# Loading v in two transfers of 64 rows instead of one from a two-block source, in a fused RWKV and convolutional FFN kernel

## The chip, the cores and the metric

One core of a Trainium2 chip. The metric is the device time of one execution in microseconds (us). Three runs of the kernel before gave 355.97, 357.77 and 359.85 us, median 357.77.

## What is computed

For 4 batches and 8 heads of width 48, over 768 steps, a linear attention with a state of 48x48 per head; its output, 384 wide, then goes through a gated FFN with a convolution of three taps along the sequence:

```python
for t in range(S):
    kt, vt, rt = (k[:, :, t], v[:, :, t], r[:, :, t])
    cur = np.einsum('bhd,bhe->bhde', u[None] * kt, vt)
    y[:, :, t] = np.einsum('bhd,bhde->bhe', rt, state + cur)
    state = w[None, :, :, None] * state + np.einsum('bhd,bhe->bhde', kt, vt)
...
h = np.maximum(x @ w_in, 0.0)
conv_out += conv_w[k][None, None, :] * hp[:, k:k + S, :]     # k = 0, 1, 2
gate = 1.0 / (1.0 + np.exp(-conv_out))
return (h * gate @ w_out).astype(np.float32)
```

## The kernel before

The sequence is cut into 24 groups of 128 steps (6 for each batch), a group into two chunks of 64. Each group g is first prepared (`prep`): DVE scales k and r of the group in `KR` by tables of decay powers that stand in PSUM (`TKR`, a view of `PO[2]`, built once at the start); for groups below 11 PE makes a token-major copy of k (line 453) which ACT puts into `TOK` (line 463), and sums for the diagonal (line 461); from group 11 on (`NE`) that copy comes from HBM as `krt` and POOL or DVE multiply it. From group 11 (`GP`) the scaling reads `TKS`, a copy of the tables in SBUF made once by ACT (line 376; the trace calls that tile TKR).

Then comes a visit (`visit`, lines 488 to 560). On PE it makes the masked scores of the next group (line 516, into `SP`), the state update k by v of the next group (line 525, into `UP`) and the outputs of this group (lines 521 and 527, into `AV`). So line 525 needs v of group g+1 in `TOK`, line 527 v of group g. After a visit DVE masks the scores and adds the states, POOL multiplies the states by the decay (`MM`), and ACT and DVE split the output in a high and a low part into `XT` (line 555 and the `tt` behind it). From group 3 on six small DMAs of 16 rows each move a part of `XT` from partition to partition.

The FFN goes over 7 units of up to 462 columns, 8 slices of 128 hidden rows each: 9 matmuls a slice for the first layer (line 585), relu, convolution, gate and split on ACT, DVE and POOL (lines 591 to 602), and 9 for the second (line 626). The first slice needs the first three groups. The weights come as 64-bit words that ACT, DVE and POOL turn to floats in 16 pieces of 384 KB and one small one (`convert`, three buffers `ST`); these are spread over the first unit.

The order of all instructions is made before the launch by a planner (`Plan`): each operation is given with an engine, an estimated duration, what it reads and writes and, for a DMA, an estimate `x` of the transfer. The planner works its own due times out and emits one fixed order for each engine; it also puts in dummy matmuls on `wz` (line 699). On the chip each engine goes through its order and waits in place. Nearly all DMAs are issued from one queue, SP's, so a DMA that waits holds up every one behind it; three loads of `KR` at the start are issued by ACT.

The loads of a group are made by `load`: two transfers for `KR` (k and r, 64 or 48 rows each), from group 11 on one for `krt` (384 KB), and one for v of 192 KB. In HBM v of a group lies in a block of 128 rows with zeros in two of four quarters, so the 128 rows that are wanted start at two places: rows 0 to 63 in the first half of the columns and rows 64 to 127 in the second. The source is therefore written by hand as an access pattern of three steps, 2 blocks by 64 rows by 384 elements, while the destination is 128 rows by 384 elements.

Of the kernel before, what the change touches and what calls it, by code (L numbers as in the profile page):

```python
# [14 lines left out]
B, H, S, D = 4, 8, 768, 48  # L15
DM, DF = 384, 1024
C = 64
NP = H // 2
# [43 lines left out]
class Plan:  # L62
# [11 lines left out]
    def op(self, eng, dur, rd, wr, fn, cls="", x=0.0, port=False, mode=0, dma=False):  # L74
        n = len(self.ops)
        self.dma.append(dma)
        pred = set()
        for k in rd:
            if k in self.last_w:
                pred.add(self.last_w[k])  # L80
        for k in wr:
            if k in self.last_w:
                pred.add(self.last_w[k])
            pred.update(self.last_r.get(k, ()))
        for k in rd:
            self.last_r.setdefault(k, []).append(n)
        for k in wr:
            self.last_w[k] = n
            self.last_r[k] = []
        pred.discard(n)  # L90
        if not isinstance(dur, dict):
            dur = {eng: dur}
        cls = cls or (wr[0] if isinstance(wr[0], str) else wr[0][0])
        self.ops.append((dur, x, sorted(pred), fn, cls, mode))
        self.port.append(port)
        return n
# [134 lines left out]
def rwkv_ffn_kernel(tc, krd, krt, vt, wd, ut, w_in, conv_w, w_out, out):  # L231
    nc = tc.nc
    V, A, G, SP, PE = nc.vector, nc.scalar, nc.gpsimd, nc.sync, nc.tensor
    plan = Plan()
    op = plan.op
    with ExitStack() as ctx:
# [3 lines left out]
        def sb(shape, dt, name, n=None):  # L240
            if n is None:
                return cst.tile(shape, dt, name=name)
            return [cst.tile(shape, dt, name=f"{name}{i}") for i in range(n)]
# [3 lines left out]
        TOK = sb([128, 3, NP, 2, D], F32, "TOK", NBUF)  # L247
        SC = sb([128, NP, 2, C], F32, "SC", 2)
# [17 lines left out]
        TKS = sb([112, 2, NP, C], F32, "TKR")  # L266
# [9 lines left out]
        TKR = PO[2][0:112].rearrange("q (a p t) -> q a p t", a=2, p=NP)  # L276
# [17 lines left out]
        def dma(rd, wr, dst, src, dur=0.5, x=0.1, cls="", q="sp"):  # L294
            op(q, dur, rd, wr, lambda e: e.dma_start(dst, src), cls, x, dma=True)  # L295
# [11 lines left out]
        def kr(i):  # L307
            return [(n, i, x) for n in ("KK", "RR") for x in range(2)]
# [3 lines left out]
        def load(g, q="sp"):  # L312
            i = g % NBUF
            dst = KR[i].rearrange("q a p t -> q (a p t)")
            n = 64 if g < NBUF else D
            dma([], [(n_, i, 0) for n_ in ("KK", "RR")], dst[0:n], rows[g * 112 + 64:g * 112 + 64 + n], 0.45, 0.63, "ldK")
            dma([], [(n_, i, 1) for n_ in ("KK", "RR")], dst[64:64 + D], rows[g * 112:g * 112 + D], 0.45, 0.63, "ldK", q)
            if g >= NE:
                dma([], [("tK", i), ("tR", i)], TOK[i][:, 0:2], krt[g], 0.45, 1.3, "ldT")
            a = vt[g]  # L320
            v = bass.AP(a.tensor, a.offset, [[(64 * 2 + 1) * NP * 2 * D, 2], [2 * NP * 2 * D, 64], [1, NP * 2 * D]])
            dma([], [("tV", i)], TOK[i][:, 2].rearrange("q p c d -> q (p c d)"), v, 0.45, 0.65, "ldV")

        load(0, "act")
        dma([], ["uu"], uu, ut, 0.45, 0.4, "ldU")
        op("pool", 0.1, [], ["ident"], lambda e: G.memset(ident, 1.0))
# [23 lines left out]
        TKK = ["TK1", "TK2", "TR1", "TR2"]  # L350
# [22 lines left out]
        op("pool", 0.6, ["w64", "ident"], ["D64"], lambda e: G.tensor_tensor(  # L373
            out=D64, in0=ident.unsqueeze(1).broadcast_to([112, NP, D]), in1=w64.broadcast_to([112, NP, D]), op=ALU.mult))
        op("pe", 0.4, ["uu", "eye"], ["AV"], ucol, "ucol", 100, mode=1)
        op("act", 0.55, TKK, ["TKS"], lambda e: A.copy(TKS, TKR), "TKS")
        su_ = AV.rearrange("q p c t -> q (p c t)")[0:112, 0:NP].unsqueeze(2)
        op("dve", 0.2, ["AV", "PW"], ["uw"], lambda e: V.tensor_tensor(out=uw.unsqueeze(2), in0=su_, in1=PW[:, :, 1:2], op=ALU.mult))

        def decays():  # L380
            op("dve", 0.6, ["PW", "PW0"], ["PL"], powers2)
            op("act", 0.32, ["PL"], ["DN"], lambda e: A.copy(DN, PL[:, :, ::-1]))
            op("pe", 0.4, ["DN", "ident"], ["SUs"], th, "th", 350, mode=1)
            op("act", 0.4, ["SUs"], ["TH"], lambda e: A.copy(TH, SP_.rearrange("q p c t -> q (p c t)")[:, 0:NP * D].rearrange("q (p d) -> q p d", p=NP)))
# [100 lines left out]
        def state(n):  # L485
            return ST_[n % 4]

        def visit(g, av, su):
            i, j = g % NBUF, (g + 1) % NBUF
            gj = (g + 1) % GPB  # L490
            rd, wr = [], []
            first = av and g % GPB == 0
            direct = g < NX
            if av:
                rd += [("SC", g % 2), ("tV", i), ("S", (2 * g + 1) % 4)] + kr(i) + ([] if first else [("S", 2 * g % 4)])
                wr += ["AV"]
            if su:
                rd += kr(j) + [("tK", j), ("tV", j)]
                wr += ["SUs", "SUu"]

            def outs(c, p):
# [27 lines left out]
            if su:  # L529
# [5 lines left out]
                for c in range(2):  # L535
# [3 lines left out]
                    a, b = state(n + c), state(n + c + 1)  # L539
# [7 lines left out]
            if av:  # L547
                b, gi = divmod(g, GPB)
                a = COLS * (b % 2) + gi * GT + (1 if b % 2 == 0 else 0)
# [94 lines left out]
        prep(0)  # L644
        conv_piece()
        visit(-1, False, True)
        for g in range(1, NBUF):
            load(g, "act" if g < 3 else "sp")
        done = [0]

        def visits(n):
            while done[0] < n:
                g = done[0]
                if g + 1 == NE:
                    decays()
                if g in SPLIT:
                    visit(g, True, False)
                if g + 1 < NG:
                    prep(g + 1)
                if g in SPLIT:  # L660
                    visit(g, False, True)
                else:
                    visit(g, True, g + 1 < NG)
                if g + NBUF < NG:
                    load(g + NBUF)
                done[0] += 1
# [9 lines left out]
        for f in range(2):  # L676
            w_in_piece(f)
        visits(UNITS[0][1])
        for u in range(NU):
            a, b = UNITS[u][1], UNITS[u + 1][1] if u + 1 < NU else NG  # L680
            for f in range(NF):
                i = u * NF + f
                first(i)
                if i >= LAG:
                    behind(i - LAG)
                if u == 0 and f + 2 < NF:
                    w_in_piece(f + 2)
                if u == 0:
                    w_out_piece(f)
                if b > a:  # L690
                    visits(min(b, a + (b - a) * (f + 2) // 7))
# [71 lines left out]
```

## Time and profile before

| | |
|---|---|
| runs of the kernel before, us | 355.97, 357.77, 359.85 (median 357.77) |
| the profiled execution, us | 360.75 |
| its span in the trace, us | 358.7 |
| mean granted clock of TensorE | 0.916 |
| instructions | 11184 |

The profiled execution took 360.75 us, of which the trace covers a span of 358.7; 2.05 us lie around it. It was 2.98 us above the median of the three runs. In the views the engines are PE (TensorE), PEld (its weight loads), DVE (VectorE), ACT (ScalarE), POOL (GpSimd) and SP, whose queue issues DMAs (SPq). Where a line belongs to a helper (292 is the helper for two-operand arithmetic, 295 the one for every DMA) the name of the tile tells which operation it is.

### The profile page before, as it was taken

The numbers are of one execution on the slowest core, as the hardware profiler recorded it, in microseconds if no ns is written. First come the engines' busy times: TensorE is split into PE (matmuls) and PEld (weight loads), VectorE is DVE, ScalarE is ACT, GpSimd is POOL, SyncE is SP. The second block draws the span as 40 slices with busy tenths as digits, with TensorE's granted clock in tenths as the row PEclk, the third lists the DMA queues.
The fourth block names the chain that finished last, engine by engine and source line by source line (L and its number), as shares of the span: only waits on it lengthen the run. The fifth ranks groups of instructions, "written<-read, shape, count | busy, mean of one in ns | idle before, by whom it ended". The sixth has DMA issues, their size and how long they took to land.

```text
span 358.7 us, 11184 instructions
## 1 busy us (share of the span) xinstructions
PE 323.8 (90%) x4817; PEld 282.2 (79%) x4817; DVE 230.4 (64%) x372; ACT 174.6 (49%) x351; POOL 141.7 (40%) x157
## 2 busy tenths in 40 slices
PE   7499998977859999869999797999999999999993
PEld 4488887857758888758988686887988888889993
DVE  5234427958964756993878786669878764555551
ACT  3003117757854454443445355335464565666662
POOL 3001326735743362874452876444531021122320
PEclk9655579996996999998999999899999999999998
DMA  7442334573441513435524435244220002001001
GB/s 136 114 124 86 106 106 123 153 206 103 155 134 42 162 34 115 119 98 152 154 69 108 121 104 174 55 116 119 79 92 13 16 5 90 0 2 53 26 2 65
DMA packets 21297, 33.46 MB, mean 93 GB/s; under 512 B 4864, under 2 KB 15168, under 8 KB 21248
## 3 DMA queue, kind: packets, MB, share of 16 engines
q1 hardware_dynamic: 20960, 32.15, 30.8%
q10 hardware_dynamic: 288, 0.59, 0.8%
q8 instruction: 38, 0.62, 0.7%
q14 instruction: 11, 0.09, 0.1%
HBM read 25.95 MB, written 4.72 MB: 85 GB/s over the span
## 4 chain that ended last, share of the span: by engine, by line
PE 57%; DMA 18%; DVE 7%; POOL 6%; issue 5%; ACT 4%; SPq 2%; POOLq 0%; ACTq 0%
PE HP L585 20%; PE PO L626 20%; DMA TOK<-in_krt_dram 6%; DMA TOK<-in_vt_dram 5%; PE SP L516 4%; PE AV L527 3%; PE AV L521 3%; POOL TOK L292 2%; DVE ST L406 2%; DMA ST<-in_w_out_dram 2%; PE UP L525 2%; DMA ST<-in_w_in_dram 2%; SPq L295 2%; PE HP L461 1%; DVE CV L595 1%
## 5 line engine op out<-in xcount | busy, mean ns | idle before, releaser
L585 PE MATMUL HP<-XT,wi 128*128 128x464 f32 (+2 forms) x504 | 117.5, 379 | 8.2 <-DMA XT<-XT 3.6
L626 PE MATMUL PO<-GG,wo 128*128 128x462 f32 (+2 forms) x504 | 115.9, 371 | 6.1 <-POOL GG L292 4.8
L585 PEld LDWEIGHTS HP<-XT,wi 128*128 128x128 f32 x504 | 95.1, 196 | 18.8 <-DMA XT<-XT 3.8
L626 PEld LDWEIGHTS PO<-GG,wo 128*128 128x128 f32 x504 | 93.3, 191 | 18.3 <-POOL GG L292 6.4
L595 DVE SCALAR_TENSOR_TENSOR CV<-HP,cw,CV 128x462 f32<-128x462 f32 (+2 forms) x112 | 75.0, 670 | 33.5 <-ACT CV L592 32.7
L292 POOL TENSOR_TENSOR GG<-CV,GG 128x462 fp32r<-128x462 f32 (+2 forms) x35 | 39.7, 1135 | 71.9 <-ACT GG L601 61.0
L591 ACT ACTIVATE HP<-HP 128x464 f32<-128x464 f32 (+2 forms) x56 | 29.3, 523 | 54.6 <-PE HP L585 54.3
L527 PE MATMUL AV<-SC,TOK 64*48 64x64 f32 (+1 forms) x816 | 55.2, 235 | 0.0
L516 PE MATMUL SP<-KR 48*64 48x64 f32 x768 | 50.5, 244 | 3.6 <-ACT QQ L470 3.6
L599 DVE TENSOR_TENSOR CV<-HP,CV 128x462 f32<-128x462 f32 (+2 forms) x56 | 34.2, 611 | 28.6 <-ACT CV L598 28.3
L521 PE MATMUL AV<-KR,SS 48*48 48x64 f32 (+1 forms) x744 | 51.4, 235 | 0.9 <-issue 0.9
L516 PEld LDWEIGHTS SP<-KR 48*64 48x64 f32 x768 | 41.8, 147 | 10.7 <-issue 4.5
L525 PE MATMUL UP<-TOK 64*48 64x48 f32 x704 | 44.6, 218 | 4.6 <-DMA TOK<-in_vt_dram 4.6
L598 ACT ACTIVATE CV<-CV 128x462 f32<-128x462 f32 (+2 forms) x56 | 31.9, 569 | 27.2 <-DVE CV L595 27.1
L527 PEld LDWEIGHTS AV<-SC,TOK 64*48 64x48 f32 (+1 forms) x816 | 41.2, 132 | 0.4
L525 PEld LDWEIGHTS UP<-TOK 64*48 64x48 f32 x704 | 36.7, 136 | 5.2 <-issue 5.2
L521 PEld LDWEIGHTS AV<-KR,SS 48*48 48x48 f32 (+1 forms) x744 | 37.0, 130 | 2.5 <-issue 1.9
L601 ACT CAST GG<-CV 128x462 fp32r<-128x462 f32 (+2 forms) x56 | 31.1, 556 | 13.5 <-DVE CV L599 13.2
L292 POOL TENSOR_TENSOR MM<-SS,w 112x192 f32<-112x192 f32 x30 | 19.7, 657 | 42.1 <-DVE SS L292 22.9
L592 ACT ACTIVATE CV<-HP,cw 128x462 f32<-128x462 f32 (+2 forms) x56 | 35.2, 628 | 2.1
L292 POOL TENSOR_TENSOR TOK<-TOK 128x384 f32<-128x384 f32 x13 | 13.6, 1049 | 48.5 <-DMA TOK<-in_krt_dram 48.5
L555 ACT CAST XT<-AV 112x512 fp32r<-112x512 f32 (+1 forms) x24 | 13.8, 575 | 26.7 <-PE AV L527 26.1
(86 smaller groups left out, 335.0 us busy)
## 6 DMA issues: line engine op xcount, KB each, us to landing
KR<-in_krd_dram SPq DMA_DIRECT2D x41, 192.0 KB
TOK<-in_krt_dram SPq DMA_DIRECT2D x13, 384.0 KB
TOK<-in_vt_dram SPq DMA_DIRECT2D x24, 192.0 KB
ST<-in_w_in_dram SPq DMA_DIRECT2D x8, 384.0 KB
ST<-in_w_out_dram SPq DMA_DIRECT2D x8, 384.0 KB
XT<-XT SPq DMA_DIRECT2D x126, 16.0 KB
out_dram<-OS SPq DMA_DIRECT2D x6, 193.0 KB
out_dram<-OS SPq DMA_DIRECT2D x6, 191.0 KB
```

Source lines behind the costliest of these rows:

```text
L292: op(eng, d, rd, wr, lambda e: e.tensor_tensor(**kw), cls, port=not psum)
L516: PE.matmul(SP_[xs[x], p, c], KK[j][rows[x], p, t], RR[j][rows[x], p, t], start=True, stop=True)
L521: PE.matmul(o, state(2 * g + c)[rows[x]].rearrange("q p d -> q (p d)")[:, sc], RR[i][rows[x], p, t], start=True, stop=False)
L525: PE.matmul(UP[rows[x], n:n + D], TOK[j][xs[x], 0, p, c], TOK[j][xs[x], 2, p, c], start=True, stop=True)
L527: PE.matmul(o, TOK[i][xs[x], 2].rearrange("q p c d -> q (p c d)")[:, vc], SC[g % 2][xs[x], p, c], start=first and c == 0, stop=True)
L585: PE.matmul(hp, wi[a][:, j, fs], src(x, j), start=(j == 0 and k == 0), stop=(j == 2 and k == 2))
L592: op("act", act(n, 0, 1), [H_, "cw"], [("T", ti)], lambda e: A.activation(t1, hp[:, 1:n + 1], AF.Copy, scale=cw[:, 3 * f + 1:3 * f + 2]), ...
L595: op("dve", dve(n, psum=1) + 0.02, [H_, "cw"], [("T", ti)], lambda e, k=k: V.scalar_tensor_tensor(out=t1, in0=hp[:, k:n + k], scalar=cw[:, ...
L598: op("act", act(n, 1), [], [("T", ti)], lambda e: A.activation(t1, t1, AF.Sigmoid), "SG")
L599: op("dve", dve(n), [H_], [("T", ti)], lambda e: V.tensor_tensor(out=t1, in0=hp[:, 1:n + 1], in1=t1, op=ALU.mult), "GG")
L601: op("act", act(n, 1), [("T", ti)], [("GH", gi)], lambda e: A.copy(gh, t1), "GH")
L626: PE.matmul(po[:, :n], wo[a][:, f, ms], g2[x], start=(f == 0 and j == 0), stop=(f == NF - 1 and j == 2))
```

## The change

`load` issues v as two transfers of 64 rows, one for each block, each with a plain two-step source; their keys in the planner are two (`("tV", i, 0)` and `("tV", i, 1)`), their estimates 0.3 each instead of one 0.65, and a visit depends on both. The copy of the decay tables to SBUF (`TKS`) is taken out of the set-up and is given to the planner when group 3 is about to be prepared, with the scaled `KR` of group 2 among what it reads.

```diff
-            a = vt[g]
-            v = bass.AP(a.tensor, a.offset, [[(64 * 2 + 1) * NP * 2 * D, 2], [2 * NP * 2 * D, 64], [1, NP * 2 * D]])
-            dma([], [("tV", i)], TOK[i][:, 2].rearrange("q p c d -> q (p c d)"), v, 0.45, 0.65, "ldV")
+            for x in range(2):
+                xs = slice(x * C, (x + 1) * C)
+                dma([], [("tV", i, x)], TOK[i][xs, 2], vt[g, xs, x], 0.45, 0.3, "ldV")
...
-        op("act", 0.55, TKK, ["TKS"], lambda e: A.copy(TKS, TKR), "TKS")
...
-                rd += [("SC", g % 2), ("tV", i), ("S", (2 * g + 1) % 4)] + kr(i) + ([] if first else [("S", 2 * g % 4)])
+                rd += [("SC", g % 2), ("tV", i, 0), ("tV", i, 1), ("S", (2 * g + 1) % 4)] + kr(i) + ([] if first else [("S", 2 * g % 4)])
...
-                rd += kr(j) + [("tK", j), ("tV", j)]
+                rd += kr(j) + [("tK", j), ("tV", j, 0), ("tV", j, 1)]
...
+                if g + 1 == 3:
+                    op("act", 0.55, TKK + kr(2), ["TKS"], lambda e: A.copy(TKS, TKR), "TKS")
```

The first piece is the order of SP's queue at the start of the program, up to the fourth load of v (KR0 to KR3 hold k and r of groups 0 to 3, TOK0 to TOK3 their v, ST the weight words):

```order
 L295 DMA uu_101<-in_ut_dram 128x192
-L295 DMA TOK0_65<-in_vt_dram 128x1x384
 L295 DMA KR1_62<-in_krd_dram 64x1024
-L295 DMA TOK1_66<-in_vt_dram 128x1x384
+L295 DMA TOK0_65<-in_vt_dram 64x384 x2
+L295 DMA TOK1_66<-in_vt_dram 64x384 x2
 L295 DMA KR2_63<-in_krd_dram 64x1024
-L295 DMA TOK2_67<-in_vt_dram 128x1x384
+L295 DMA TOK2_67<-in_vt_dram 64x384 x2
```

Each load of v is two rows, and the load of group 1's k and r stands ahead of the first v instead of behind it.

The second piece is again SP's queue, in the middle of the program, where `krt` is loaded too and `XT<-XT` are the small moves of the output:

```order
-L295 DMA TOK1_66<-in_vt_dram 128x1x384
+L295 DMA TOK1_66<-in_vt_dram 64x384 x2
+L295 DMA XT_79<-XT_79 16x2x128 x6
 L295 DMA TOK2_67<-in_krt_dram 128x768
+L295 DMA KR2_63<-in_krd_dram 48x1024 x2
+L295 DMA TOK2_67<-in_vt_dram 64x384 x2
+L295 DMA TOK3_68<-in_krt_dram 128x768
 L295 DMA XT_79<-XT_79 16x2x128 x6
-L295 DMA KR2_63<-in_krd_dram 48x1024 x2
-L295 DMA TOK2_67<-in_vt_dram 128x1x384
-L295 DMA XT_79<-XT_79 16x2x128 x6
-L295 DMA TOK3_68<-in_krt_dram 128x768
```

One set of six moves goes ahead of a load of `krt`, another one that stood ahead of such a load goes behind it, and a load of `krt` is issued right behind the two halves of v.

The third and fourth pieces are ACT's order at the start, before and then after (TKR is the copy to SBUF, PO2 the tables in PSUM):

```order
L371 COPY PO2_125<-PO2_125 112x4x32
L376 COPY TKR_111<-PO2_125 112x512
L382 COPY DN_110<-PL_107 112x256
L463 COPY TOK0_65<-HP0_121 128x384
```

After the change:

```order
L371 COPY PO2_125<-PO2_125 112x4x32
L381 COPY DN_110<-PL_107 112x256
L462 COPY TOK0_65<-HP0_121 128x384
L541 COPY SS1_72<-UP_119 112x192
L462 COPY TOK1_66<-HP1_122 128x384
L401 ACTIVATE ST1_97<-ST1_97 128x384
L404 ACTIVATE ST1_97<-ST1_97 128x384
L554 CAST XT_79<-AV_120 128x3x128
L462 COPY TOK2_67<-PO1_124 128x384
```

The copy to SBUF is gone from the start; it comes some ten operations later on ACT. On PE the order is the same up to the visit of group 12, after which visits and FFN slices change places by a slice or two.

## Rows read from the trace of the kernel before

**Rows 1.** The page: busy time of each engine; granted clock in 40 slices, in tenths.
```profile
PE 323.8 (90%) x4817; PEld 282.2 (79%) x4817; DVE 230.4 (64%) x372; ACT 174.6 (49%) x351; POOL 141.7 (40%) x157
...
PEclk9655579996996999998999999899999999999998
```

**Rows 2.** Timeline, 0 to 30 us: start, us, engine, line, operation [idle before <-releaser].
```profile
8.80 0.33 PE L516 MATMUL SP<-KR 48*64 48x64 f32 x4
...
13.70 0.40 PE L525 MATMUL UP<-TOK 64*48 64x48 f32 x4 [4.57 <-DMA TOK<-in_vt_dram]
...
14.68 1.28 DVE L292 TENSOR_TENSOR KR<-KR,PO 112x512 f32<-112x512 f32 x2 [6.59 <-DMA KR<-in_krd_dram]
```

**Rows 3.** Timeline of SP's queue, and the loads of v as a group.
```profile
2.50 0.65 SPq L295 DMA_DIRECT2D TOK<-in_vt_dram  x1
...
4.85 5.45 SPq L295 DMA_DIRECT2D KR<-in_krd_dram  x1
...
10.94 5.09 SPq L295 DMA_DIRECT2D KR<-in_krd_dram  x2
...
17.14 6.39 SPq L295 DMA_DIRECT2D ST<-in_conv_w_dram  x1
...
L295 SPq DMA_DIRECT2D TOK<-in_vt_dram x24: 522/578/912, 2.5 to 254.1; - x24
```

**Rows 4.** Stretches: length, busy us of each engine, clock, DMA share, GB/s.
```profile
2.00:4.00 2.00, 2.00 (x6) 0.73 (x5) 1.41 (x6) 0.86 (x1) 1.19 (x8) 1.00 0.58 152
4.00:6.00 2.00, 1.85 (x6) 0.49 (x4) 0.94 (x3) 1.89 (x7) 0.35 (x1) 1.00 1.15 228
9.00:10.00 1.00, 0.13 (x4) 0.00 (x0) 0.00 (x0) 0.00 (x0) 0.00 (x0) 1.00 0.13 38
13.00:14.00 1.00, 0.30 (x7) 0.33 (x8) 0.00 (x0) 0.00 (x0) 0.00 (x0) 0.50 0.13 41
34.00:35.00 1.00, 1.00 (x35) 0.83 (x35) 0.00 (x0) 0.00 (x0) 0.00 (x0) 0.50 0.13 49
```

**Rows 5.** Stretches of the start: PE, PEld, DVE, ACT, POOL busy, clock, DMA.
```profile
9.00:13.70 4.70, 0.13 (x4) 0.03 (x1) 0.00 (x0) 0.00 (x0) 0.00 (x0) 0.80 0.32 90
14.00:18.00 4.00, 4.00 (x85) 4.00 (x83) 1.98 (x3) 0.32 (x1) 0.51 (x1) 0.50 0.61 150
18.00:49.00 31.00, 30.87 (x569) 26.38 (x570) 11.07 (x20) 5.37 (x14) 6.17 (x8) 0.50 0.37 107
49.00:53.50 4.50, 4.50 (x143) 4.09 (x139) 1.77 (x4) 0.48 (x1) 0.78 (x2) 0.96 0.36 92
```

**Rows 6.** The chain that ended last: 32 matmuls of a preparation (start, us, what).
```profile
40.88 1.78 PE HP L453 x32
...
119.65 1.06 PE SP L453 x32
```

**Rows 7.** The same chain: transfers, from their issue to the work they release.
```profile
72.66 7.23 DMA ST<-in_w_in_dram
...
83.28 2.88 DMA ST<-in_w_out_dram
...
97.36 4.72 DMA ST<-in_w_out_dram
...
156.97 4.87 DMA XT<-XT
...
188.29 7.33 DMA TOK<-in_krt_dram
```

**Rows 8.** Stretches behind the start, columns as in the other stretches.
```profile
72.00:126.00 54.00, 43.73 (x716) 38.40 (x716) 37.50 (x57) 31.86 (x71) 24.50 (x25) 0.87 0.44 132
126.00:244.00 118.00, 108.12 (x1818) 93.30 (x1818) 85.22 (x133) 54.51 (x103) 66.76 (x66) 0.97 0.39 111
244.00:351.00 107.00, 105.59 (x1029) 95.00 (x1027) 70.95 (x117) 62.70 (x119) 27.77 (x29) 1.00 0.13 39
```

## Prediction

> **What bounds the kernel now.** I read the page first: PE is busy for 323.8 of 358.7 us [rows 1], so the end moves only with PE's idle time (34.9 us) or with the clock it is granted. The clock line shows where that is not full: 9655579 at the start, then 6, 6, 8 and 8 among nines [rows 1]. So I went to the start, and there to the timeline. PE issues its last score matmuls at 8.80 for 0.33 us, then stands idle to 13.70, for 4.57 us, until the first v has landed; DVE stands for 6.59 us, to 14.68, for k and r of group 1, which SP issues behind that v [rows 2]. SP itself is stuck: three issues take 5.45, 5.09 and 6.39 us where a load of v is normally issued in 0.58 [rows 3].
>
> Why are transfers so late when the HBM has little to do? The stretches of one microsecond answer it [rows 4]. While loads of v are all that is left to move, the DMA share stays at 0.13 and the rate at 38 to 49 GB/s; the same plateau comes three times here. One engine of 16 is 0.0625 of the share, so 0.13 is two engines. Loads of k and r, 64 or 48 rows each, drive it to 1.15 and 228 GB/s [rows 4]. So a load of v, 192 KB, runs on two engines, and at 49 GB/s it takes 3.9 us; whatever else has rows on those two engines waits behind it. SP's stuck issues fit this: 16.93 us for four issues that should take 2.3.
>
> [...]
>
> The consequence on the clock is in the stretches of the start [rows 5]: the mean is 0.80 over PE's idle time, then 0.50 from 14 to 49 us, with PE busy for 34.87 of 35.0 us, and 0.96 from 49 on. [...] PE did 0.13 us of work in the 4.7 us in which the clock fell. So the wait for v costs far more than its own 4.6 us.
>
> **The change, part by part.**
>
> First term, the wait for the first v. Up to and with it the new order moves 448 KB of k and r of group 0, 96 of u, 448 of group 1, 192 of group 2 (from ACT's queue) and 192 of v: 1376 KB. From 2 to 4 us 304 KB move, then 228 KB a us [rows 4]: (1376 - 304) / 228 = 4.7, so v is there at about 8.7 us, group 1's k and r sooner. PE comes to it at 9.13 [rows 2]. I take 4.2 of the 4.57 us off, leaving 0.4 for the notice of the landing; the bounds are 0 and 4.57.
>
> Second term, the clock. If PE no longer stands, I see nothing at 9 us that would take the clock down, and the 35 us at 0.50 shrink. By the clock alone they halve, which is 17.4 us saved. The rows for one shape at both levels give a little less: 32 matmuls of a preparation take 1.78 us at 40.88 and 1.06 at 119.65, a ratio of 0.60, so 14.0 saved [rows 6]. I take the middle, 15.7. But DVE has 13.05 us of work between 14 and 49 [rows 5] that no clock of PE shortens, and part of it stands between the end of one visit and the start of the next; 3 us come back as new idle time of PE. That leaves 13, with bounds 0 (the clock falls all the same) and 17.4. What is late next there is DVE, with the masks and states of the visits.
>
> Third term, transfers later on. On the chain, 384 KB of weights take 2.88 us from issue to work at 83.28; but 7.23 at 72.66, right behind a load of v, and 4.72 at 97.36. A move of only 16 KB takes 4.87 at 156.97, and `krt`, 384 KB, takes 7.33 at 188.29 and twice more about as long [rows 7]. Excess over 2.88: 4.35 and 1.84 for the weights; at most the 3.9 us of one load of v for the move; and for the three `krt` 3.9 each at most, since k and r are ahead of them as well. That is 4.35 + 1.84 + 3.9 + 11.7 = 21.8 us that two engines can have cost. It reaches the end only as far as PE suffers: from 72 to 244 us PE is idle for 10.27 and 9.88 us, and a clock of 0.87 and 0.97 costs 43.73 x 0.13 + 108.12 x 0.03 = 8.9 [rows 8], so 29 us at most. Of the 21.8 I take somewhat over half, 12, since DVE (85.22 of 118 us) and POOL (66.76) are the next to be waited for [rows 8]. The bounds are 0 and 21.8. From 244 to 351 PE is busy for 105.59 of 107 us at clock 1.00 [rows 8]: nothing is to be had there.
>
> What is added: 24 issues on SP at 0.58 us [rows 3], 13.9 us. At the start the three stuck issues give back 14.6 of SP's time, more than the whole change adds, so I charge nothing there. Later an issue puts 0.6 us before what stands behind v on SP's queue: the 13 loads of `krt`, whose first user is POOL, and the moves of the output, for which PE waits at 157. That price is at most 13 x 0.58 = 7.5 us, at least 0; since the load ahead is shorter by about 3 us each time, I count it as paid inside the third term. If those transfers do not get shorter, the 7.5 stand alone (the rival on the other side).
>
> The copy of the tables moves from 5.4 us on ACT to some ten operations later. DVE's first scaling starts as that copy ends, so up to 0.6 us could be won, if k and r of group 0 are there by then; ACT has 5.69 us of work from 14 to 49 [rows 5], so the copy costs nothing where it goes. I take 0. The changed order on PE from group 12 on I also take at 0, with 3 us either way.
>
> Sum: 4.2 + 13 + 12 = 29.2 us, from 360.75 to 331.6. The profiled execution stands 3 us above the median of the runs; I put the forecast at 330, between 331.6 and 328.6.
>
> [...]
>
> **Rivals.**
>
> The clock falls anyway. PE has other short waits in the first 50 us, such as for group 1's k and r or for DVE between visits, and once the clock was down 35 us of busy PE did not bring it back [rows 5]. For it: the clock stayed down through all of that work. Against it: from 49 to 53.5 the same kind of work ran at 0.96, and before 9 us the clock was full [rows 4, 5]. Then the second term is 0: 360.75 - 4.2 - 12 = 344.6, or 343 on the runs' level.
>
> The start's gain is given back in the first FFN unit. The 16 weight pieces are converted by ACT and DVE, which use 31.86 and 37.50 of 54 us from 72 to 126 [rows 8], and some of it is done while PE is late at the start. If the conversion sets the pace, the first two terms vanish and the third stays: 360.75 - 12 = 348.8, about 347. Against it: these engines are at 59% and 69%, not full.
>
> The change does not do what it says: the halves run on few engines too, or another transfer holds the same instructions up. Then nothing moves, 358. Against it are the loads of k and r, also 64 rows, at a share of 1.15 [rows 4].
>
> Slower: the two halves follow one another and land no sooner than the one did, and the second issue delays each of the 13 `krt` behind it by 0.58 us. Then 357.8 + 7.5 = 365. The place is SP's queue at `krt`; it decides if the landing of `krt` after its issue stays at 7.3 us.
>
> **Chances.** The forecast, 330 with a range of its own of 318 to 341, has 0.56. The clock falling anyway has 0.22, the gain given back 0.12, no change 0.05, slower 0.05. The range that leaves no more than 2 in 10 out reaches from the far end of the first (all three terms near their upper bounds, 360.75 - 4.57 - 17.4 - 21.8 = 317) to the two middle cases with some 3 us of disorder above them, 350. About 1%, 3.6 us, is what a measurement of this kernel can tell from no change, as its three runs spread over 3.9. The first three cases are all faster by more: 0.90; within 1%: 0.05; slower by more: 0.05.
>
> **What would show it.** First step: no stretch with a DMA share of 0.13 while v is loaded, no issue of several us on SP, and PE waiting for v at 9 us for well under 1 us. Second: a clock of 1.00 through 9 to 35 us and the first FFN matmul (line 585) at about 36 instead of 53.5 us; a clock of 0.50 there makes the first rival right. Third: `krt` and weights landing within 3 to 5 us of their issue, PE's idle time between 72 and 244 us down from 20.2 to about 12. If the 0.13 stays, or the first FFN matmul comes before 40 us and the end does not follow, the forecast is wrong.

## The result and the profile after

Four runs of the changed kernel took 328.12, 331.78, 340.22 and 340.74 us, median 336.0; four of the kernel before, beside them, 355.97 to 359.85, median 358.32: faster by 22 us in the medians. The ratio is 0.921, its 95% interval 0.909 to 0.934; the ratios here and below leave out every run more than 1.5% above the fastest of its kernel. The forecast was 330, its range 317 to 350. The four runs are no single cluster, and what parts them is the mean clock that TensorE was granted: 0.934 and 0.933 in the two near 340, 0.961 and 0.981 in the two near 330. The profiled execution is one of the upper pair: 340.22 us, span 338.5, of which 358.7 - 338.5 = 20.2 us are gone.

The page of the kernel after, busy times, the granted clock in 40 slices, and DMA issues (count, KB each, median us from issue to landing):

```profile
PE 319.1 (94%) x4817; PEld 278.8 (82%) x4817; DVE 235.2 (69%) x372; ACT 173.8 (51%) x351; POOL 139.9 (41%) x157
...
PEclk9955599979769999969999999999999999999999
...
TOK<-in_krt_dram SPq DMA_DIRECT2D x13, 384.0 KB, 3.5
TOK<-in_vt_dram SPq DMA_DIRECT2D x48, 96.0 KB, 3.1
```

PE has 319.1 us of work against 323.8 [rows 1] and stands for 19.4 us in place of 34.9. The clock line still has its fives at the start. `krt` lands a median 3.5 us after its issue; three before took 7.33 and about as much, from issue to the work they release [rows 7]. The waits (us in all, times, longest), of the kernel before and then of the kernel after, say the same:

```profile
POOL TOK L292 <- DMA TOK<-in_krt_dram: 48.5, 12, 8.0
...
POOL TOK L292 <- DMA TOK<-in_krt_dram: 22.4, 9, 3.6
```

Next the timeline of PE in the kernel after (columns as in [rows 2]; a line number is one lower than before):

```profile
8.94 0.33 PE L515 MATMUL SP<-KR 48*64 48x64 f32 x4
10.16 0.43 PE L524 MATMUL UP<-TOK 64*48 64x48 f32 x3 [0.89 <-DMA TOK<-in_vt_dram]
...
15.98 0.51 PE L460 MATMUL HP<-uw,SC 48*64 48x1 f32 x12 [0.50 <-issue]
```

The stand of 4.57 us [rows 2] is one of 0.89: v is there at about 10.0 and PE goes on at 10.16, not at 13.70. The queue of SP at the same place:

```profile
3.02 3.52 SPq L295 DMA_DIRECT2D TOK<-in_vt_dram  x4
6.59 0.59 SPq L295 DMA_DIRECT2D KR<-in_krd_dram  x1
```

The first four halves take 3.52 us to issue, 0.88 each, where single issues of before took up to 6.39 [rows 3]. The stretches of the kernel after (columns: the stretch, its length, busy us and count of PE, PEld, DVE, ACT and POOL, granted clock, DMA share, GB/s):

```profile
9.00:10.00 1.00, 0.27 (x5) 0.13 (x4) 1.00 (x2) 0.00 (x0) 0.00 (x0) 1.00 1.06 240
13.00:14.00 1.00, 1.00 (x35) 0.95 (x33) 0.79 (x2) 0.00 (x0) 0.12 (x1) 1.00 1.09 238
...
16.00:17.00 1.00, 1.00 (x32) 0.95 (x32) 0.39 (x1) 0.00 (x0) 0.00 (x0) 1.00 1.20 247
17.00:18.00 1.00, 1.00 (x32) 0.86 (x28) 0.90 (x2) 0.24 (x1) 0.00 (x0) 0.51 0.74 268
18.00:40.00 22.00, 21.87 (x427) 18.52 (x423) 7.60 (x14) 4.97 (x14) 5.67 (x7) 0.50 0.33 84
72.00:126.00 54.00, 50.60 (x862) 45.18 (x863) 41.18 (x60) 31.88 (x69) 28.24 (x29) 0.88 0.41 119
126.00:244.00 118.00, 114.31 (x1802) 99.22 (x1804) 98.26 (x151) 59.26 (x112) 65.64 (x66) 0.97 0.41 115
```

The plateau at a share of 0.13 [rows 4] is gone: 1.06 and 1.09 at 240 and 238 GB/s in the two stretches shown of the start's loads. The clock holds at 1.00 until 17 us, falls there, and is 0.50 from 18 to 40 while PE is busy for 21.87 of 22 us. From 72 to 244 us PE stands for 7.1 us, before for 20.2, while the clock there is what it was, 0.88 and 0.97 beside 0.87 and 0.97 [rows 8].

A point that splits the program well is the first FFN matmul. It came at 53.5 us before and comes at 45.6 now:

```profile
L584 PE MATMUL HP<-XT,wi x504: 332/372/725, 45.6 to 326.5; 128*128 128x464 f32 x96, 128*128 128x384 f32 x48, 128*128 128x468 f32 x24
```

So of the 20.2 us, 7.9 were won before it, and 12.3 behind it (305.2 to 292.9 from that matmul to the end). Below, "start" is the time of this matmul, "rest" what follows it to the end of the span.

### The profile page after: what moved, and what is told of

Read it like the earlier page. It is cut to its first block, busy times and chain, and to the rows that moved or that the text cites. A ratio compares the mean times of both kernels' runs of the same rounds, so it can differ in the third digit from the quotient of the medians.

```text
span 338.5 us, 11224 instructions
## 1 busy us (share of the span) xinstructions
PE 319.1 (94%) x4817; PEld 278.8 (82%) x4817; DVE 235.2 (69%) x372; ACT 173.8 (51%) x351; POOL 139.9 (41%) x157
## 4 chain that ended last, share of the span: by engine, by line
PE 78%; DVE 7%; DMA 7%; ACT 3%; issue 2%; SPq 1%; POOL 1%; POOLq 0%; ACTq 0%
PE HP L584 28%; PE PO L625 27%; PE SP L515 5%; PE AV L526 4%; PE AV L520 4%; PE UP L524 2%; DMA TOK<-in_vt_dram 2%; DMA ST<-in_w_out_dram 2%; DVE ST L405 2%; PE SP L452 1%; SPq L295 1%; PE SP L460 1%; DVE CV L594 1%; DMA ST<-in_w_in_dram 1%; PE HP L460 1%
## 5 line engine op out<-in xcount | busy, mean ns | idle before, releaser
L584 PE MATMUL HP<-XT,wi 128*128 128x464 f32 (+2 forms) x504 | 116.1, 376 | 4.9 <-DMA XT<-XT 3.4
L292 POOL TENSOR_TENSOR GG<-CV,GG 128x462 fp32r<-128x462 f32 (+2 forms) x32 | 36.9, 1155 | 68.9 <-ACT GG L600 62.0
L526 PE MATMUL AV<-SC,TOK 64*48 64x64 f32 (+1 forms) x816 | 54.1, 232 | 0.0
L520 PE MATMUL AV<-KR,SS 48*48 48x64 f32 (+1 forms) x744 | 50.5, 233 | 0.0
L515 PE MATMUL SP<-KR 48*64 48x64 f32 x768 | 48.9, 239 | 1.5 <-ACT QQ L469 1.5
L598 DVE TENSOR_TENSOR CV<-HP,CV 128x462 f32<-128x462 f32 (+2 forms) x56 | 34.2, 613 | 22.7 <-ACT CV L597 22.5
L515 PEld LDWEIGHTS SP<-KR 48*64 48x64 f32 x768 | 40.6, 143 | 8.4 <-issue 4.9
L524 PE MATMUL UP<-TOK 64*48 64x48 f32 x704 | 43.1, 213 | 0.9 <-DMA TOK<-in_vt_dram 0.9
L526 PEld LDWEIGHTS AV<-SC,TOK 64*48 64x48 f32 (+1 forms) x816 | 40.4, 130 | 0.3
L524 PEld LDWEIGHTS UP<-TOK 64*48 64x48 f32 x704 | 35.6, 131 | 1.6 <-issue 1.5
L292 POOL TENSOR_TENSOR MM<-SS,w 112x192 f32<-112x192 f32 x35 | 20.8, 594 | 33.8 <-DVE SS L292 25.6
L292 POOL TENSOR_TENSOR SC<-eye,QQ 128x512 f32<-128x512 f32 x19 | 21.9, 1151 | 29.4 <-PE AV L526 21.5
```

What stands on the lines that cost most here:

```text
L292: op(eng, d, rd, wr, lambda e: e.tensor_tensor(**kw), cls, port=not psum)
L515: PE.matmul(SP_[xs[x], p, c], KK[j][rows[x], p, t], RR[j][rows[x], p, t], start=True, stop=True)
L520: PE.matmul(o, state(2 * g + c)[rows[x]].rearrange("q p d -> q (p d)")[:, sc], RR[i][rows[x], p, t], start=True, stop=False)
L524: PE.matmul(UP[rows[x], n:n + D], TOK[j][xs[x], 0, p, c], TOK[j][xs[x], 2, p, c], start=True, stop=True)
L526: PE.matmul(o, TOK[i][xs[x], 2].rearrange("q p c d -> q (p c d)")[:, vc], SC[g % 2][xs[x], p, c], start=first and c == 0, stop=True)
L584: PE.matmul(hp, wi[a][:, j, fs], src(x, j), start=(j == 0 and k == 0), stop=(j == 2 and k == 2))
```

## The experiments

Two theories at first. **Engines**: the old load ran on two DMA engines, because its source has two blocks, and all that counts is on how many engines it runs. **Order**: the planner emits another order with the change (first v behind group 1's `KR`, moves and `krt` elsewhere), or the moved copy does it.

| kernel | what it is | median of runs, us | kernel before, us | start, us | rest, us |
|---|---|---|---|---|---|
| before | | 360.75 in the profile | | 53.5 | 305.2 |
| after | | 336.0 | 358.32 | 45.6 | 292.9 |
| after_again | the change once more | 335.91 | 359.42 | 39.8 | 290.9 |
| one128 | v one plain load of 128 rows | 336.78 | 359.42 | 48.5 | 286.1 |
| halves2 | halves, each of two blocks | 367.34 | 359.42 | 53.7 | 311.8 |
| one4 | one load of four blocks | 346.19 | 359.42 | 53.5 | 291.8 |
| split_only | the split without the moved copy | 333.9 | 361.3 | 38.5 | 292.9 |
| tks_only | the moved copy without the split | 361.89 | 361.3 | 54.3 | 307.4 |
| start128 | plain load for the first four groups | 359.09 | 361.3 | 51.5 | 305.0 |
| rest128 | plain load for all but those | 340.77 | 361.3 | 53.5 | 285.9 |
| late_one | one128, some loads issued later | 327.28 | 361.84 | 40.4 | 286.1 |
| late_after | after, the same loads later | 334.37 | 361.84 | 37.8 | 293.7 |
| dummy_after | after, dummy matmuls at the start | 339.36 | 361.84 | 40.1 | 289.2 |
| late_dummy_one | both on one128 | 332.76 | 361.84 | 41.6 | 287.2 |

Start and rest are from the one profiled execution of each; the medians are of all runs.

### On how many engines v is loaded

after_again is the changed kernel as it is, for its spread. 

> The changed kernel once more, for its spread and for a profile in which the clock may hold. Theory A (the number of engines that carry v is what changed): 328 to 341 us, no stretch with a DMA share of 0.13 while v is loaded. The clock theory adds: where the clock stays at 1.00 from 9 us on, the first FFN matmul comes at 30 to 38 us and the run takes 326 to 333; where it falls, at 44 to 47 us and 338 to 342. Rival (the order of instructions brings the gain): the same total, so this run alone does not tell the two apart.

It took 332.39, 332.61, 339.22 and 342.3 us (mean clock 0.973, 0.967, 0.938, 0.934), ratio 0.930 (0.913 to 0.946). Its profiled execution is one at 332.61, and the stretches of its start read otherwise:

```profile
8.00:12.00 4.00, 4.00 (x67) 3.33 (x65) 2.38 (x4) 0.48 (x1) 0.00 (x0) 0.58 1.08 237
12.00:29.00 17.00, 16.48 (x526) 14.11 (x522) 9.61 (x18) 5.46 (x14) 4.97 (x7) 1.00 0.56 145
29.00:36.00 7.00, 6.66 (x107) 5.75 (x106) 1.43 (x3) 0.58 (x3) 1.71 (x3) 0.51 0.54 141
36.00:40.00 4.00, 4.00 (x127) 3.64 (x124) 1.94 (x5) 0.48 (x2) 0.94 (x2) 1.00 0.53 128
```

Here the clock is down early, a mean of 0.58 from 8 to 12 us, and comes back: the same program is at 1.00 from 12 to 29 us and has its first FFN matmul at 39.8: 13.7 us won before it, 14.3 behind it, 28.0 together. A difference of a few us between two kernels is read with this spread in mind.

one128 keeps the kernel before, its single issue and its dependencies, and lays v out so that 128 plain rows are read:

```diff
-            v = bass.AP(a.tensor, a.offset, [[(64 * 2 + 1) * NP * 2 * D, 2], [2 * NP * 2 * D, 64], [1, NP * 2 * D]])
+            v = a[:, 0].rearrange("q p c d -> q (p c d)")
...
-        z[:, :64, 0], z[:, 64:, 1] = x[:, :64], x[:, 64:]
+        z[:, :, 0] = x
```

> The kernel before in its own order, with one transfer of v as now, but its source is 128 plain rows at the same pitch in HBM instead of two blocks of 64. Theory A: 16 engines carry v, so 326 to 341 us as with the halves, perhaps 1 to 3 us less since SP has 24 issues fewer; the share of 0.13 is gone. Rival (two smaller transfers, the planner's new order or the moved table copy bring the gain): nothing of these is in this kernel, so 355 to 361 us.

336.78 us, ratio 0.942 (0.931 to 0.953). No instruction of the kernel before was moved or added, and the gain is there. So it needs neither the split nor the new order. halves2 is the counterpart: the changed kernel with its 48 issues, each half read from two blocks (v lies in HBM in four quarters to fit).

```diff
-                dma([], [("tV", i, x)], TOK[i][xs, 2], vt[g, xs, x], 0.45, 0.3, "ldV")
+                a = vt[g, 64 * x:64 * x + 64, 2 * x]
+                v = bass.AP(a.tensor, a.offset, [[(32 * 4 + 1) * NP * 2 * D, 2], [4 * NP * 2 * D, 32], [1, NP * 2 * D]])
+                dma([], [("tV", i, x)], TOK[i][xs, 2].rearrange("q p c d -> q (p c d)"), v, 0.45, 0.3, "ldV")
```

> The changed kernel with its order and its two transfers of 64 rows, but the source of each is two blocks of 32 rows. Theory A: each half runs on two engines, 3.9 us of both for one v as before; 355 to 365 us, the upper end if the 24 more issues on SP cost what the slower rival said (7.5 us); the share of 0.13 is back. Rival (two transfers or the order bring the gain): 328 to 341 us.

367.34 us, ratio 1.023 (1.006 to 1.040). Two of its stretches:

```profile
27.00:28.00 1.00, 1.00 (x20) 0.91 (x19) 0.00 (x0) 0.00 (x0) 0.00 (x0) 0.50 0.13 49
...
126.00:244.00 118.00, 105.52 (x1695) 90.30 (x1694) 83.78 (x129) 53.29 (x101) 58.74 (x59) 0.96 0.36 102
```

Its wait for `krt`:

```profile
POOL TOK L292 <- DMA TOK<-in_krt_dram: 49.0, 11, 8.0
```

The plateau at 0.13 and 49 GB/s is back, and with it the long landings: 49.0 us of waiting, where the kernel before has 48.5 and the kernel after 22.4. PE does 105.52 us of work from 126 to 244, less than the 108.12 of before [rows 8]. The split, with the order it brings, is by itself a loss of 8 us, by the interval 2 to 14; the time is above the expected 355 to 365. one4 is the kernel before with one load whose source has four blocks of 32 rows (again with v laid out to fit):

```diff
-            v = bass.AP(a.tensor, a.offset, [[(64 * 2 + 1) * NP * 2 * D, 2], [2 * NP * 2 * D, 64], [1, NP * 2 * D]])
+            v = bass.AP(a.tensor, a.offset, [[(32 * 4 + 1) * NP * 2 * D, 4], [4 * NP * 2 * D, 32], [1, NP * 2 * D]])
```

> The kernel before in its own order, the one source of v made of four blocks of 32 rows. Theory A: four engines carry v, a plateau of the DMA share at 0.25 to 0.27 with about 98 GB/s, 2.0 us for one v instead of 3.9, PE waits for the first v till about 11 us; 336 to 350 us, between the two kernels. Rival: 355 to 361 us.

346.19 us, 13.2 below the kernel before, 9.4 above one128. One expected sign did not come: PE waits for the first v till 13.53, not 11, and the first FFN matmul stays at 53.5, so the gain in its profile lies behind the start (305.2 to 291.8).

```profile
13.53 0.40 PE L525 MATMUL UP<-TOK 64*48 64x48 f32 x4 [4.32 <-DMA TOK<-in_vt_dram]
```

Two stretches while v is loaded:

```profile
24.00:25.00 1.00, 1.00 (x28) 0.83 (x26) 0.74 (x2) 0.00 (x0) 0.00 (x0) 0.50 0.28 103
...
34.00:35.00 1.00, 1.00 (x38) 0.86 (x37) 0.00 (x0) 0.00 (x0) 0.00 (x0) 0.50 0.25 95
```

Two blocks give 0.13 and 49 GB/s, four 0.25 to 0.28 and 95 to 103: by the shares, 1/16 for one engine, the number of blocks is the number of engines here, and each moves some 24 to 26 GB/s. The engines theory stands. With halves of 64 rows no such plateau shows: the kernel after has 1.06 and 1.09, the other loads of the start included.

### The moved copy

split_only puts the copy of the tables back into the set-up of the changed kernel (the edit below); tks_only moves it in the kernel before (the reverse of that edit).

```diff
+        op("act", 0.55, TKK, ["TKS"], lambda e: A.copy(TKS, TKR), "TKS")
         su_ = AV.rearrange("q p c t -> q (p c t)")[0:112, 0:NP].unsqueeze(2)
...
-                if g + 1 == 3:
-                    op("act", 0.55, TKK + kr(2), ["TKS"], lambda e: A.copy(TKS, TKR), "TKS")
```

> The two halves of v alone; the copy of the decay tables stays at the start. My theory: all of the gain is here, 328 to 342 us, as the changed kernel. Rival (the moved copy lets DVE and so PE start earlier and keeps the clock): 345 to 358 us.

> The moved copy of the decay tables alone; v by the one transfer on two engines. My theory: 355 to 361 us, as before, at most 0.6 us at the start, where DVE's first scaling began as the copy ended. Rival: 345 to 355 us.

The split alone gives 333.9 (327.91 to 340.49), the copy alone 361.89 (357.31 to 363.76) beside 361.3. The copy is worth nothing that shows; what counts in the change is the split.

### Start and rest by themselves

start128 has the plain load for the first four groups only, rest128 for all others; both on the kernel before.

```diff
             v = bass.AP(a.tensor, a.offset, [[(64 * 2 + 1) * NP * 2 * D, 2], [2 * NP * 2 * D, 64], [1, NP * 2 * D]])
+            if g < NBUF:
+                v = a[:, 0].rearrange("q p c d -> q (p c d)")
...
+        z[slice(0, NBUF), :, 0] = x[slice(0, NBUF)]
```

In rest128 the comparison is `g >= NBUF`, and the slice the other groups.

> The kernel before in its own order; only the first four loads of v (the ones before any visit is over) have a source of 128 plain rows, the other 20 stay on two engines. This is my first and second term by themselves: PE comes by v by 11 us, first FFN matmul at 40 to 49 us instead of 53.5, and 342 to 352 us. Rival (the start's gain is given back in the first FFN unit): first FFN matmul earlier, but 355 to 361 us.

> The other way round: the first four loads of v stay on two engines, the 20 later ones have a source of 128 plain rows. This is my third term by itself: the first FFN matmul stays at 52 to 54 us, PE's idle time from 72 to 244 us falls from 20 to about 10 us, and 343 to 351 us. Rival (the later transfers were hidden, all gain comes from the start): 355 to 361 us.

start128 took 358.62, 359.57, 360.57 (mean clock 0.908 to 0.920) and once 349.29 (0.949): median 359.09, 2.2 below the kernel before. The expectation missed: the first FFN matmul comes at 51.5, not at 40 to 49. The time lies where the rival put it, but not for its reason, as the start is won by 2.0 us only. Its start tells why so little:

```profile
6.92 0.52 PE L367 MATMUL AV<-eye,uu 64*48 64x1 f32 x16 [1.47 <-DMA uu<-in_ut_dram]
...
7.00:8.00 1.00, 1.00 (x35) 1.00 (x36) 1.00 (x3) 0.00 (x0) 0.00 (x0) 0.80 1.13 242
9.00:13.70 4.70, 4.70 (x71) 3.98 (x73) 1.98 (x3) 0.48 (x1) 0.00 (x0) 0.50 1.06 226
```

From 9 us on PE no longer stands, 4.70 us of work in 4.70, but at a clock of 0.50, where the kernel before had a mean of 0.80 over the same stretch [rows 5]. The wait for v is gone, yet the clock was down before it: it fell between 7 and 8 us, behind an earlier wait of PE, 1.47 us for `uu`. rest128 took 340.77, 20.5 below and a little under the expected 343 to 351. Its stretches:

```profile
72.00:126.00 54.00, 48.27 (x805) 41.87 (x808) 42.77 (x61) 34.69 (x77) 29.17 (x29) 0.94 0.49 138
126.00:244.00 118.00, 117.99 (x2069) 102.91 (x2061) 97.97 (x159) 62.62 (x118) 73.73 (x71) 1.00 0.45 125
```

Its first FFN matmul comes at 53.5 as before. From 126 to 244 PE stands for 0.01 us, at full clock. Idle time from 72 to 244 falls from 20.15 to 5.74, which is 14.4; what the clock costs there falls from 8.9 to 48.27 x 0.06 = 2.9, which is 6.0; together 20.4, where the profiled execution is 19.3 shorter (358.7 to 339.4): the whole gain. In the medians the two parts add up: 2.2 + 20.5 = 22.7, and one128, which has both, won 22.6. That they meet so closely is in part chance: in the profiled executions it is 2.2 + 19.3 = 21.5 beside 24.1, as the clock at the start falls at another time in each.

### What holds the start

In one128 PE stops in the midst of 32 matmuls of one form, the sums of group 1. Its timeline:

```profile
13.56 0.74 PE L461 MATMUL HP<-uw,SC 48*64 48x1 f32 x20
17.16 0.81 PE L461 MATMUL HP<-uw,SC 48*64 48x1 f32 x12 [2.85 <-issue]
```

"issue" means that it waited for nothing that the profile shows. The kernel after has a stop at the same place, after the same 20 matmuls, of 0.50 us. The stretches of one128 around it:

```profile
14.25:14.30 0.05, 0.05 (x3) 0.00 (x0) 0.05 (x1) 0.00 (x0) 0.00 (x0) 0.96 1.29 184
14.30:14.35 0.05, 0.01 (x2) 0.00 (x0) 0.05 (x1) 0.00 (x0) 0.00 (x0) 0.50 2.07 307
...
14.00:15.00 1.00, 0.31 (x12) 0.22 (x8) 0.66 (x2) 0.00 (x0) 0.04 (x1) 0.65 0.99 195
15.00:16.00 1.00, 0.00 (x0) 0.00 (x0) 0.00 (x0) 0.00 (x0) 0.00 (x0) 0.50 1.01 363
16.00:17.00 1.00, 0.00 (x0) 0.00 (x0) 0.00 (x0) 0.00 (x0) 0.00 (x0) 0.50 1.03 378
17.00:18.00 1.00, 0.83 (x16) 0.84 (x18) 0.00 (x0) 0.52 (x1) 0.00 (x0) 0.50 0.07 25
```

PE goes on just as the DMA share falls from 1.03 to 0.07, with the clock down. But it is not this stop that took the clock down: it fell at 14.30, in the moment in which the stop begins. The DMA queues of one128 from 14 to 15 us (packets, MB, share):

```profile
q1 hardware_dynamic: 59, 0.18, 90.4%
q8 instruction: 1, 0.02, 8.3%
```

That packet of the instruction queue is the only one from 12 to 18 us. So a new pair of theories: **instructions late** (it takes PE's next instructions to come by that queue, whose packet stands beside the loads, 8.3% and 90.4% of the engines, and to wait while these are full), or **the clock needs work** (PE's short waits take it down, and dummy matmuls would hold it). late_one issues the loads of group 3 and the first two weight pieces later, from ACT, behind the preparation of group 1; late_after does the same in the changed kernel. The edit of late_one, in part:

```diff
+            z, rd = ("act", [("tK", 1)]) if g == 3 else ("sp", [])
...
+            dma(rd, [("tV", i)], TOK[i][:, 2].rearrange("q p c d -> q (p c d)"), v, 0.45, 0.65, "ldV", z)
...
+            dma([("tK", 1)] if q == "act" else [], [kl, kh], st, src, 0.45, n / 300.0, "wdma", q)
...
+                if g == 0:
+                    load(3)
+                    for f in range(2):
+                        w_in_piece(f, "act")
...
-        for f in range(2):
-            w_in_piece(f)
```

> As one128 (one transfer of v from 128 plain rows, the tables' copy at the start), but the loads of group 3 and of the first two weight pieces are issued by ACT behind its copy for group 1 instead of early on SP. Theory C (the start is full of transfers, PE's own instructions come late through them, and that stop takes the clock down): the DMA share is well under 1.00 from 12 to 15 us, PE's stop of 2.85 us inside the 32 matmuls of group 1's sums shrinks to under 0.5, the clock holds beyond 14 us, first FFN matmul at 38 to 43 us instead of 48.5, 324 to 333 us. Rival D (the stop has nothing to do with the loads): it stays, 335 to 339 us as one128.

> The changed kernel with the same later loads. Theory C: the runs gather at the lower end of the changed kernel's 328 to 342, 324 to 333 us, as PE's stops near 15 us go. Rival D: the same spread, 328 to 342 us.

dummy_after adds 8, 4 and 6 dummy matmuls at the start of the first three visits; late_dummy_one has both edits on one128.

```diff
             def mm(e):
+                for _ in range({-1: 8, 0: 4, 1: 6}.get(g, 0)):
+                    PE.matmul(PO[0][:, :FN], wz[:, :128], wz[:, :FN], start=True, stop=True)
```

> The changed kernel with 18 more dummy matmuls of 256 columns (2.4 us of PE at full clock): 8 ahead of the first visit, where PE waits for v, 4 and 6 ahead of the next two. Theory C in its weaker form (any idle time of PE in the first 40 us can take the clock down): the clock holds at 1.00 from 9 to 30 us in the profile, first FFN matmul at 36 to 41 us, 326 to 333 us in nearly all runs. Rival D: the clock falls as often, and 330 to 345 us.

> Later loads and dummy matmuls together, on one128: the candidate for the fastest. Theory C: 322 to 331 us. Rival D: 336 to 342 us.

late_one is the fastest kernel of the study: 327.28 us (325.37 to 331.98), ratio 0.905 (0.896 to 0.913). No run of it is as slow as any of one128 (336.68 to 337.16). Its timeline, at the sums of group 1, where one128 stopped:

```profile
15.75 1.09 PE L462 MATMUL HP<-uw,SC 48*64 48x1 f32 x32
```

Its stretches:

```profile
8.00:12.00 4.00, 4.00 (x81) 3.49 (x79) 2.52 (x6) 0.48 (x1) 0.00 (x0) 0.68 1.02 216
12.00:14.00 2.00, 2.00 (x62) 2.00 (x60) 0.47 (x1) 0.44 (x2) 0.36 (x1) 0.78 0.13 31
14.00:29.00 15.00, 14.42 (x467) 12.27 (x466) 8.76 (x16) 3.85 (x9) 3.88 (x7) 1.00 0.56 158
```

Its queues from 12 to 13 us (packets, MB, share):

```profile
q1 hardware_dynamic: 147, 0.05, 20.0%
q8 instruction: 1, 0.02, 6.9%
```

The 32 matmuls run unbroken, and the instruction packet falls where other transfers take 20%. The clock is down early, a mean of 0.68 from 8 to 12 us, comes back, and is 1.00 from 14 to 29 us. The first FFN matmul comes at 40.4, 8.1 before that of one128; the rest, 286.1 us, is the same.

So the later loads bring some 9 us, and the signs of theory C came. That full DMA engines by themselves make the stop is not borne out by two other profiles. In after_again the same 32 matmuls run unbroken at a share of 1.05, and split_only stops for 0.95 us, again with "issue", where nothing is moved:

```profile
15.35 1.10 PE L460 MATMUL HP<-uw,SC 48*64 48x1 f32 x32
15.00:16.00 1.00, 1.00 (x26) 0.78 (x26) 0.99 (x2) 0.18 (x1) 0.36 (x1) 1.00 1.05 264
...
20.10 0.26 PE L527 MATMUL AV<-SC,TOK 64*48 64x64 f32 x2 [0.95 <-issue]
19.00:20.00 1.00, 0.15 (x11) 0.03 (x2) 0.00 (x0) 0.00 (x0) 0.00 (x0) 1.00 0.00 0
```

In the changed kernel the edit brings less: 334.37 (328.68 to 335.34) beside medians of 336.0 and 335.91, within the spread, so the expected 324 to 333 missed. The dummies did not help in the medians: 339.36 without and 332.76 with the later loads, 5.5 above late_one and between the ranges of the two theories. The profiled execution of dummy_after does show what theory C promised, a clock of 1.00 up to 30 us and the first FFN matmul at 40.1:

```profile
9.00:30.00 21.00, 19.98 (x593) 17.23 (x592) 11.72 (x22) 5.73 (x14) 5.12 (x7) 1.00 0.65 158
```

But it is the fastest of four, 331.21; the others took 336.29 to 345.26 at mean clocks of 0.959 to 0.930. Shown is that the time falls in one128 when these loads come later, by ACT's queue instead of SP's, and that the stop is gone from its profile. What makes PE stop is not shown; that its instructions come late is inferred from the one packet and from "issue". Nor is it shown what takes the clock down at the start.

## Why the prediction was right, and where its sizes were off

**The cause.** The step from 0.13 to two engines is right, and tested from three sides (one128, halves2, one4). That 64 rows run on more than two engines stood on the 1.15 of the loads of k and r [rows 4]; the start of the kernel after shows 1.06 and 1.09. All promised signs of this step came, but two in part: PE's wait for v is 0.89 us, not well under 1, and SP's issues at the start are shorter, not all free.

**First term, 4.2 us for the first v.** Measured 13.70 - 10.16 = 3.5. It was mis-sized by 0.7: v landed at about 10.0 and not at 8.7. By 10.0 us 1570 KB had moved (157 GB/s over the first 10 us), not the 1376 of the sum, so other loads went along with it; the issues of the first four halves were stretched to 3.52 us too. The 0.4 us for the notice of the landing was an estimate; in both profiles PE goes on 0.14 us after it (13.57 to 13.70 before, 10.03 to 10.16 after).

**Second term, 13 us for the clock.** This is the term that was mis-sized in the profiled execution: the start came down by 7.9, of which 3.5 are the first term, so 4.4 are left for the second. The step that failed there is "if PE no longer stands, I see nothing at 9 us that would take the clock down, and the 35 us at 0.50 shrink". At 9 us that held (1.00 until 17); then the clock fell, 1.0 us after the end of a stop of 0.50 us. The trace of before shows no such stop: there the same 32 matmuls run unbroken:

```profile
21.64 1.87 PE L461 MATMUL HP<-uw,SC 48*64 48x1 f32 x32
```

In start128 and after_again the clock was down before 9 us already. By the prediction's own sign, a clock of 0.50 between 9 and 35 us, the first rival, "the clock falls anyway", was right in the profiled execution. In after_again and split_only the start came at 39.8 and 38.5: 13.7 and 15.0 won of the 17.2 that the two terms promised. split_only shows the size best, as its clock is nearly full, a mean of 0.92 from 18 to 40 us:

```profile
14.00:18.00 4.00, 4.00 (x113) 3.38 (x114) 2.63 (x5) 0.83 (x2) 0.51 (x1) 1.00 0.95 249
18.00:40.00 22.00, 20.46 (x565) 17.53 (x562) 10.12 (x20) 6.22 (x17) 7.92 (x10) 0.92 0.47 121
```

Its PE went on at 10.04, which is 3.7 of the first term and leaves 11.3 for the second, near the 13. So the term is right in some runs and the first rival in others: it gave 343, and the upper runs of the kernel lie at 339 to 342; the others lie at 328 to 333, around the 330 of the forecast. None of the eight runs lies between 333 and 339. That the median, 336.0, comes within 6 us of the forecast is in part luck: it is the middle of two groups, and 7 from the rival.

**Third term, 12 us for later transfers.** Its net is right, 12.3 in the profiled execution and 14.3 in after_again, but by two errors that cancel, which is luck. "Of the 21.8 I take somewhat over half" was too little: rest128 won 20.5 (19.3 in its profile), nearly all of the 21.8, and DVE and POOL did not take PE's place. And the price, "paid inside the third term", is real: with halves and the planner's new order the rest takes 289.2 to 293.7 (five kernels, mean 291.9), with one plain load 285.9 to 287.2 (four kernels, mean 286.3; two of them in the order of before, two with the later loads). So 5.6 us are given back in these profiles, one for each kernel, of the at most 7.5 that the prediction named. Whether it is the 24 issues or the order that came with them was not told apart, and stays open.

**The rivals.** The start's gain is not given back in the first FFN unit: late_one starts the FFN 8.1 us before one128, and both have a rest of 286.1. "No change" fell with the 0.13. The slower one, 365, came near: halves2, in which the halves land no sooner, took 367.34, 7.9 over the kernel before (2 to 14 by the interval); its condition, that `krt` goes on landing late, is seen in its 49.0 us of waiting. That the loss is the delay of `krt`, as the rival has it, is not shown: POOL waits for it only 0.5 us longer than in the kernel before.

**Two transfers or one.** The one transfer of before ran on two engines by its share of 0.13, so the split won 22 us. Once the single load reads plain rows, as in one128, the split has no lead that shows: 336.0 against 336.78 in the median, and the rest is shorter for the single load, 286.1 against 292.9.

## What to carry to other kernels

A stretch in which the DMA share stayed flat at a small multiple of 1/16, 0.13 in the kernel before, with SP stuck in issues of up to 6.39 us, was here the sign of a transfer on few engines; the larger part of its price was the lateness of other transfers, 20.5 us in rest128 beside 2.2 in start128. Count the blocks of the source's access pattern (two gave 0.13, four 0.25 to 0.28), and lay the source out so that one transfer has plain rows, before splitting it: in one128 that brought 22.6 us without an added issue. A saving that rests on the clock of TensorE was a bet with two outcomes here; give each its number, and look at every wait of PE around it, the ones before the wait that goes away too.

## What was not expected of the hardware

PE stopped in the midst of a run of equal matmuls, for 2.85 us in one128 and 0.50 us in the changed kernel, with nothing in the profile that it waited for; with fewer transfers in that stretch, in late_one, the stop was gone, though after_again had none at a share of 1.05. One program ran at 0.50 from 18 to 40 us in one execution and at 1.00 from 12 to 29 in another, and the eight runs of it fall into two bunches, 328 to 333 us with a mean clock of 0.96 or more and 339 to 342 with 0.93 to 0.94. A busy PE does not tell the two apart: it was busy for 21.87 of 22 us at 0.50 in the first, while in late_one, busy for 4.00 of 4 us at a mean of 0.68 from 8 to 12, it was back at 1.00 by 14 us. And without PE's wait at 9 us the clock did not always stay up: in start128 PE was busy throughout 9 to 13.7 us at 0.50, as it had fallen between 7 and 8 us.
